# Attention and FFN on one core: q and k loaded onto the two partition halves, nine tokens a row, and turned as 64x64 tiles

## The chip, the cores and the metric

The kernel runs on one core of a Trainium2 chip. The metric is the time of one execution on the device, in microseconds. The kernel before takes 364.85 us (median of 3 runs, 364.39 to 365.44).

## What is computed

```python
B, H, S, D = 8, 8, 576, 64                       # batch, heads, tokens, head size
scores = matmul(q, k.transpose(0, 1, 3, 2)) / sqrt(D)
scores = scores + bias[None]                     # by the distance of two tokens, from a 32 x 8 table
attn = exp(scores - max) / sum(...)
x = matmul(attn, v)                              # then heads side by side: 4608 tokens x 512
h = x @ w_in                                     # 512 -> 2048
out = maximum(0.01 * h, h) @ w_out               # 2048 -> 512
```

Inputs and output are float32; the kernel works in bf16 with float32 sums.

## The kernel before

**Items.** The attention is done in 32 items, numbered n = 0 to 31: one batch and one pair of heads each, four items a batch. The FFN is done in nine groups of 512 tokens. As soon as a batch's four items have left their rows in `xT`, pieces of the FFN are put between the steps of later items, so TensorE has matmuls of both kinds in its queue.

**Loading q and k.** `load_qk` (L119) takes float32 rows of q or k from memory into bf16 tiles `qn` and `kn` with a DMA from GpSimd's queue. A partition holds six consecutive tokens of each head (`RQ = 96` rows, `NC = 6` tokens a row), so q fills partitions 0 to 95 of `qn`, and k partitions 0 to 95 of `kn`. There are two buffers of each, for even and odd batches.

**Turning q and k.** The scores need q and k with the head size on the partitions: `qt` and `kt`, 128 partitions (two heads of 64) by 576 tokens. That is done in three ways:

- Items 0 to 5: `turned_pair` (L280) lets TensorE turn each head's 96x64 block by itself, `L292`: six blocks of two heads, 12 small matmuls for q and 12 for k. The two heads of a block land on the two halves of the PSUM partitions.
- Items 6 to 8: `pair_rows` (L265) has VectorE put the two heads of a row beside each other, one copy of 96x768 for q and one for k (`L270`), and TensorE turns 96x128 blocks, `L288`: six matmuls for q and six for k.
- Items 9 to 31: `pair_rows` makes the same two copies, and `turn_by_dma` (L276) turns the whole 96x1536 tile with one DMA transpose from SyncE's queue into `tu`.

After that VectorE or ScalarE copies the turned block into `qt` or `kt` (`L307`, `L313` out of PSUM; `L319`, `L326` out of `tu`); these copies read with a step, so that tokens come out in order. Then come the scores (`L354`, `L347`, `L357`, `L358`), the exponentials on ScalarE (`L373` and others), the product with the table's band on VectorE (`L408`, `L401`), the products with v (`L421`, `L432`, `L476`), the division by the sum (`L452`, `L454`) and the turning of the result into `xT` (`L490`, or a DMA transpose). FFN matmuls are `L532`, `L584`, `L720` and `L845`.

**What sets the order.** The instructions of each engine run in the order in which the program issues them. For items 0 to 7 that order is written out by hand in the string `first` (L1115): a token `tk 6` turns k of item 6, `tq 6` turns q, `rows 6` makes item 6's two copies of `L270`, `ac 4 1 0` is one piece of item 4's product with v. Later items follow `body_in_halves` (L739), then `body_in_lanes` (L915); there `rows_ahead` (L1101) makes the copies of `pair_rows` two or three items ahead.

Of the kernel before, what the change touches and what calls it, by code (L numbers as in the profile page):

```python
# [11 lines left out]
BF16 = mybir.dt.bfloat16  # L12
# [25 lines left out]
def kernel(  # L38
# [17 lines left out]
    P = 128  # L56
    n_pairs = H // 2
# [22 lines left out]
    ps_m_pool = ctx.enter_context(tc.tile_pool(name="ps_m", bufs=2, space=bass.MemoryType.PSUM))  # L80

    ident = per.tile([P, P], BF16, name="ident")
# [8 lines left out]
    hk4 = per.tile([P, n_pairs, P + SL], BF16, name="hk4")  # L91

    NBUF = 2
    RQ = 96
    NC = S // RQ
    qn = [per.tile([P, H, NC, D], BF16, name=f"qn{i}") for i in range(NBUF)]
    kn = [per.tile([P, H, NC, D], BF16, name=f"kn{i}") for i in range(NBUF)]
    vn = [per.tile([P, NJ, H, D + 1], BF16, name=f"vn{i}") for i in range(NBUF)]
    v4 = [per.tile([P, n_pairs, D + 1], BF16, name=f"v4_{i}") for i in range(NBUF)]
    kts_ = [per.tile([P, S + P], BF16, name=f"kt{i}") for i in range(2)]  # L100
# [17 lines left out]

    def load_qk(b, h0, h1, which=("q", "k")):  # L119
        i = b % NBUF  # L120
        for name, src, dst in (("q", q, qn[i]), ("k", k, kn[i])):
            if name not in which:
                continue
            nc.gpsimd.dma_start(
                out=dst[0:RQ, h0:h1, :, :].rearrange("r h c d -> r h (c d)"),
                in_=src[b, h0:h1, :, :].rearrange("h (r c) d -> r h (c d)", c=NC),
            )

# [62 lines left out]
    for j, (u, lo, w, m) in enumerate(groups):  # L191
        copy = nc.scalar.copy if j % 2 else nc.vector.tensor_copy
        copy(out=ub[:, C0 + lo : C0 + lo + m * w].rearrange("h (m w) -> h m w", w=w),
             in_=e8[:, u : u + m].unsqueeze(2).to_broadcast([H, m, w]))
    row = ub[:, :]
    nc.vector.tensor_copy(
        out=ub[:, C0 - BAND + 1 : C0],
        in_=bass.AP(tensor=row.tensor, offset=row.offset + C0 + BAND - 1,
                    ap=[list(row.ap[0]), [-1, BAND - 1]]),
# [56 lines left out]
    items = [(b, p) for b in range(B) for p in range(n_pairs)]  # L256
# [6 lines left out]
    prs, turned = {}, {}  # L263

    def pair_rows(n):  # L265

        b, p = items[n]
        t = prs[n] = pr_pool.tile([RQ, 2, NC, 2 * D], BF16, name="pr")
        for j, src in enumerate((qn, kn)):
            nc.vector.tensor_copy(out=t[:, j, :, :].rearrange("r c (e d) -> r c e d", e=2),  # L270
                                  in_=src[b % NBUF][0:RQ, 2 * p : 2 * p + 2, :, :].rearrange("r e c d -> r c e d"))

    def by_dma(n):
        return n > 2 * n_pairs

    def turn_by_dma(n):  # L276
        t = turned[n] = tu_pool.tile([P, 2 * NC, RQ], BF16, name="tu")
        nc.sync.dma_start_transpose(out=t, in_=prs.pop(n).rearrange("r j c d -> r (j c d)"))

    def turned_pair(n, j):  # L280

        if by_dma(n):
            return turned[n][:, j * NC : (j + 1) * NC, :].rearrange("p c r -> p r c")
        ps = ps_m_pool.tile([P, 8 * P], BF16, name="ps_t", tag="m")
        b, p = items[n]
        for c in range(NC):
            if n > n_pairs + 1:
                nc.tensor.transpose(ps[:, c * RQ : (c + 1) * RQ], in_=prs[n][:, j, c, :],  # L288
                                    identity=ident[0:RQ, 0:RQ])
                continue  # L290
            for e in range(2):
                nc.tensor.transpose(ps[e * D : (e + 1) * D, c * RQ : (c + 1) * RQ],  # L292
                                    in_=(qn, kn)[j][b % NBUF][0:RQ, 2 * p + e, c, :],
                                    identity=ident[0:RQ, 0:RQ])
        return ps[:, 0:S].rearrange("p (c r) -> p r c", c=NC)

    def apart(t):

# [182 lines left out]
    def x_by_dma(n):  # L481
        return n_pairs + 2 <= n < N - 1 and n != 2 * n_pairs - 1
# [127 lines left out]
    def can(kind):  # L610
        T = made[kind]
        if at_piece[kind]:
            return True
        if kind == "in":
            return T < made["ready"] and T < made["out"] + 2
        return T < made["in"]
# [54 lines left out]
    def plan(n):  # L671
        g = room["left"] = groups_of(n)
        room["lead"] = can("out") and g >= 8 and not can("in")
        room["split"] = can("out") and g < 8 and not can("in")
        room["only"] = can("in") and not can("out") and g < 6
        room["keep"] = 4 if can("out") and not room["lead"] else 0
# [357 lines left out]
    def finished(n):  # L1034
        b, p = items[n]
        if p == n_pairs - 1:
            while made["ready"] < n_tt and (made["ready"] + 1) * TT <= (b + 1) * S:
                made["ready"] += 1
# [73 lines left out]
    def score(n, u):  # L1112
# [16 lines left out]
        b 3 2, ac 3 0 1, ac 3 1 1, xt 2, xc 2, ac 3 1 2, m 4 0, m 4 2, fin 3, e 4 0, ac 3 0 2, ac 3 0 3,  # L1129
        ac 3 1 3, e 4 2, p0 0,  # L1130
        begin 4, m 4 3, dv 3 0.1, e 4 3, xt 3 o0, xc 3, b 4 0, p0 1, p1 0 0, p1 1 0, m 4 4 s, b 4 1, m 4 5,
        tk 5, ck 5, e 4 5, e 4 4, b 4 4, moe, ap 5, moe, b 4 5, b 4 2, rows 6, m 5 1, at 4, e 5 1, m 5 0,
        ac 4 1 0, ac 4 0 0, ac 4 0 1, ac 4 1 1, tq 6, e 5 0, ac 4 0 2, tk 6,
        begin 5, ac 4 0 3, m 5 5, ac 4 1 2, cq 6 v, dv 4 0, ac 4 1 3, m 5 2, e 5 5, dv 4 1, i m, m 5 3,
        m 5 4, ck 6, i m, sl 5 1, b 5 0, e 5 2, b 5 5, l 0, i s, xt 4, sl 5 2, i o1, rows 7, e 5 4, l 1,
        e 5 3, ap 6, i m, b 5 1, l 0, b 5 4, m 6 1, at 5, xc 4, l 0, b 5 2, ac 5 0 0, ac 5 0 1, ac 5 0 2,
        begin 6, ac 5 1 0, tq 7, l 0, ac 5 0 3, e 6 1, tk 7, m 6 0, e 6 0, dv 5 0, ac 5 1 1, ck 7,
        ac 5 1 2, ac 5 1 3, dv 5 1, i s, ap 7, sl 6 1, m 6 2, l 0, m 6 4, cq 7 v, xt 5, e 6 2, b 6 1, xc 5,
        m 6 3, i m, e 6 4, m 6 5, i o0, i o1, l 1, e 6 3, i m, e 6 5, b 6 2, m 7 1, b 6 5, l 0, m 7 0,
        at 6, b 6 4, sl 6 2,  # L1140
        begin 7, b 6 0, ac 6 0 0, ac 6 1 0, l 0, ac 6 0 1, ac 6 1 1, e 7 1, rows 8, ac 6 0 2, tk 8,
        ac 6 0 3, ac 6 1 2, ac 6 1 3, i s, dv 6 0, e 7 0, dv 6 1, l 0, i m, m 7 2, l 0, ck 8, sl 7 1,
        m 7 3, xt6, l 0, turn 7, m 7 4, o, e 7 3, e 7 2, b 7 2, tq 8, b 7 1, m 7 5, b 7 0, cq 8 a, o,
        e 7 4, ap 8, b 7 4, e 7 5, b 7 5, sl 7 2, o, o,
# [68 lines left out]
    for n in range(2 * n_pairs, N + 1):  # L1213
        live = n < N
        more = n + 1 < N
        if x_by_dma(n - 2):
            finished(n - 2)
        if kind_of(n) is not None:
            body_in_lanes(n)
            continue  # L1220
        plan(n)
        kinds = two_kinds(n)
        if kinds:
            body_in_halves(n, kinds)
            continue
        all_in = live and n > 2 * n_pairs and can("in") and not can("out") and left("in") >= 6
        if live:
            begin(n)
            ps_a, ps_b = qk_mm(n, 0), qk_mm(n, 1)
            exp(n, 0, ps_a)  # L1230
            exp(n, 1, ps_b)
        av_tails(n - 1)
        av(n - 1, 0)
        first = live and by_dma(n + 1)
        if first:
            band(n, 0)
# [24 lines left out]
        x_transposes(n - 1)
        while stores:
            o, y = stores.pop(0)
            nc.sync.dma_start(out=o, in_=y)
        if not x_by_dma(n - 1):
            finished(n - 1)
        if not live:
            break
        if room["only"]:
            band(n, 1)  # L1270
        band(n, 2)
        if room["only"]:
            if not by_dma(n + 2):
                pair_rows(n + 2)
            exp(n, 3, ps_b)
            moe(2)
            exp(n, 4, ps_c)
            score(n, 5)
            T, f = step("in")
            room["left"] -= 1  # L1280

            def last_bands():
                band(n, 5)
                band(n, 4)

            leaky(T, f, ffn_in(T, f), True, last_bands)
            moe(room["left"])
            continue
        block = moe_block(1 if all_in else None, "s" if n == 3 * n_pairs - 1 else 0)
        next(block)  # L1290
        exp(n, 3, ps_b)
        next(block)
        if not all_in:
            exp(n, 4, ps_c)
        if can("out"):
            next(block)
# [38 lines left out]
```

## Time and profile before

| | before |
|---|---|
| median of the runs | 364.85 us (364.39 to 365.44) |
| span of the profiled execution | 362.8 us |
| TensorE (PE) busy | 353.4 us, 97% |
| ScalarE (ACT) busy | 243.4 us, 67% |
| VectorE (DVE) busy | 189.5 us, 52% |
| GpSimd (POOL) busy | 107.4 us, 30% |
| DMA packets | 106429, 40.27 MB |

The span is the profiled execution's own time; around it lie 2.05 us up to the median of the runs, and the prediction takes that part as it is.

PE is a matmul and PEld the load of its weights. Times are microseconds from the start of the span unless marked ns. A matmul's duration in the trace is its passage through the array, and several are under way at once. So what a matmul costs is read from the distance between the starts of two runs of matmuls, not from its duration. In a row of the timeline the first number is the start, the second the time from the first start to the last end of a run of like instructions, and "x12" their count. A form such as 96*64 in a TensorE row is the part of the array that the instruction uses: rows * columns.

### The profile page before, as it was taken

To read this page: it belongs to the slowest core of one execution; us is meant where nothing else is said; L and a number is where in the kernel's file an instruction comes from. 1 tells how busy PE (TensorE), PEld (TensorE's weight loads), DVE (VectorE), ACT (ScalarE), POOL (GpSimd) and SP (SyncE) were. 2 spreads that over 40 slices of the span, in tenths; PEclk is the share of its full clock that TensorE was granted. 3 is DMA by queue.
4 is the path that set the end of the run, shared out by engine and by line. 5 is a ranking of instruction groups with operands and counts; after the bars stand their busy time and mean duration, and the time that the engine had idled before them with its cause. 6 is when DMAs were issued, how large, how long until landed. Compare 5 with 4: busy or idle time off the path is not lost.

```text
span 362.8 us, 12074 instructions
## 1 busy us (share of the span) xinstructions
PE 353.4 (97%) x5174; PEld 204.7 (56%) x5191; DVE 189.5 (52%) x499; ACT 243.4 (67%) x364; POOL 107.4 (30%) x195
## 2 busy tenths in 40 slices
PE   7899999999999999999999999999999999999996
PEld 3465555555556777666666665565666544444443
DVE  3796876677756767655555566556554300200000
ACT  5999888479958898777777777777776264054111
POOL 8857617254334344432243334211000000000000
PEclk8999999999999999999999999999999999999999
DMA  8999999997899899979998889875111000210212
GB/s 104 196 193 147 190 206 159 197 156 115 99 130 137 114 148 139 138 120 122 133 136 124 108 119 129 122 103 96 52 49 51 29 31 0 85 33 0 80 66 87
DMA packets 106429, 40.27 MB, mean 111 GB/s; under 512 B 83713, under 2 KB 102409, under 8 KB 106377
## 3 DMA queue, kind: packets, MB, share of 16 engines
q0 software_dynamic: 55200, 18.36, 48.4%
q1 hardware_dynamic: 49880, 19.06, 27.2%
q10 hardware_dynamic: 1296, 2.10, 1.6%
q8 instruction: 41, 0.67, 0.7%
q14 instruction: 12, 0.09, 0.1%
HBM read 37.68 MB, written 9.45 MB: 130 GB/s over the span
## 4 chain that ended last, share of the span: by engine, by line
PE 93%; DVE 3%; ACT 1%; issue 1%; DMA 1%; POOL 0%; ACTq 0%; POOLq 0%
PE pm L845 35%; PE pm L584 16%; PE pm L532 15%; PE ps_o L476 8%; PE ps_s L354 8%; PE pm L720 2%; PE ps_o L432 2%; PE ps_o L421 1%; PE ps_s L845 1%; DMA kn<-in_k_dram 1%; DVE at L408 1%; PE ps_t L292 1%; PE pm L577 1%; PE ps_s L347 1%; PE ps_s L357 1%
## 5 line engine op out<-in xcount | busy, mean ns | idle before, releaser
L845 PE MATMUL pm<-xT,w_in_sb 64*128 64x512 bf16 x608 | 142.1, 376 | 0.0
L373 ACT ACTIVATE at<-ps_s 128x1024 bf16<-128x1024 f32 x120 | 118.6, 1026 | 33.7 <-PE ps_s L354 32.1
L845 PE MATMUL pm<-w_out_sb,gt 64*128 64x512 bf16 x544 | 132.6, 376 | 0.0
L556 ACT ACTIVATE gt<-pm 128x512 bf16<-128x512 f32 x140 | 82.1, 605 | 38.8 <-PE pm L532 33.4
L408 DVE TENSOR_TENSOR at<-at,hk 128x768 bf16<-128x768 bf16 (+3 forms) x149 | 65.6, 453 | 41.6 <-ACT at L385 24.8
L845 PEld LDWEIGHTS <-w_in_sb 64*128 64x128 bf16 x608 | 50.7, 94 | 20.4 <-issue 0.7
L845 PEld LDWEIGHTS <-gt 64*128 64x128 bf16 x544 | 47.0, 94 | 22.7 <-issue 3.5
L584 PE MATMUL pm<-w_out_sb,gt 128*128 128x512 bf16 x261 | 59.0, 379 | 0.7 <-issue 0.5
L532 PE MATMUL pm<-xT,w_in_sb 128*128 128x512 bf16 x242 | 56.9, 379 | 0.5
L354 PE MATMUL ps_s<-qt,kt 64*128 64x512 bf16 x240 | 44.3, 383 | 2.3 <-ACT at L373 0.8
L584 PEld LDWEIGHTS <-gt 128*128 128x128 bf16 x268 | 25.5, 98 | 29.9
L532 PEld LDWEIGHTS <-w_in_sb 128*128 128x128 bf16 x252 | 23.7, 98 | 27.0 <-issue 0.6
L476 PE MATMUL ps_o<-vn,at 64*128 64x65 bf16 x1920 | 38.4, 190 | 0.0
L476 PEld LDWEIGHTS <-at 64*128 64x128 bf16 x1920 | 35.7, 94 | 4.6 <-issue 4.4
L131 POOL DMA_DIRECT2D vn<-in_v_dram x32 | 33.8, 1060 | 9.1 <-issue 4.2
L385 ACT ACTIVATE at<-ps_s 128x576 bf16<-128x576 f32 x30 | 19.9, 663 | 17.9 <-PE pm L845 17.9
L454 DVE TENSOR_TENSOR opair<-ps_o,rcp 128x320 bf16<-128x320 f32 x64 | 29.1, 487 | 1.1
L896 DVE COPY y<-pm 128x512 f32<-128x512 f32 x17 | 11.8, 692 | 27.7 <-PE pm L845 27.7
L597 DVE COPY y<-pm 128x512 f32<-128x512 f32 x11 | 7.6, 691 | 33.5 <-PE pm L584 30.6
L354 PEld LDWEIGHTS <-kt 64*128 64x128 bf16 x240 | 14.7, 94 | 16.7 <-issue 6.6
L1088 POOL COPY tick<-opair 1x1 bf16<-1x1 bf16 x43 | 7.9, 185 | 54.6 <-DVE opair L454 54.6
L1088 POOL COPY tick<-at 1x1 bf16<-1x1 bf16 x21 | 5.5, 263 | 61.0 <-DVE at L408 61.0
(108 smaller groups left out, 348.9 us busy)
## 6 DMA issues: line engine op xcount, KB each, us to landing
out_dram<-y SPq DMA_DIRECT2D x24, 256.0 KB, 3.7
qn<-in_q_dram POOLq DMA_DIRECT2D x28, 144.0 KB, 4.7
kn<-in_k_dram POOLq DMA_DIRECT2D x28, 144.0 KB, 3.5
vn<-in_v_dram POOLq DMA_DIRECT2D x24, 128.0 KB, 4.5
w_in_sb<-in_moe_w_in_dram POOLq DMA_DIRECT2D x4, 512.0 KB, 9.2
w_out_sb<-in_moe_w_out_dram POOLq DMA_DIRECT2D x2, 1024.0 KB, 13.4
out_dram<-y ACTq DMA_DIRECT2D x7, 256.0 KB, 2.0
vn<-in_v_dram POOLq DMA_DIRECT2D x16, 64.0 KB, 8.0
```

The lines of the kernel that those rows point to most:

```text
L131: nc.gpsimd.dma_start(out=vn[b % NBUF][:, c, h0:h1, 0:D], in_=v[b, h0:h1, c * P : (c + 1) * P, :].rearrange("h s d -> s h d"),)
L354: nc.tensor.matmul(ps[:, e, :], lhsT=kt[r, u * P : (u + 1) * P], rhs=qt[r, 0:512], start=True, stop=True)
L373: nc.scalar.activation(at[:, :, u, 0:512], ps, AF.Exp, scale=scale)
L385: nc.scalar.activation(at4[:, 0:w], ps.rearrange("p e i -> p (e i)")[:, 0:w], AF.Exp, scale=scale)
L408: nc.vector.tensor_tensor(out=o, in0=o, in1=m, op=ALU.mult)
L454: nc.vector.tensor_tensor(out=opair[:, 0:m, e * D : (e + 1) * D], in0=ps[:, :, 0:D], in1=rcp.to_broadcast([P, m, D]), op=ALU.mult)
L476: m = nc.tensor.matmul(outs[n][e][:, ic * (D + 1) : (ic + 1) * (D + 1)], lhsT=at[halves[r], o : o + P], rhs=vn[b % NBUF][halves[r], c, 2 * ...
L532: nc.tensor.matmul(pm, lhsT=w_in_sb[:, c, f * P : (f + 1) * P], rhs=xT[c][:, T * TT : (T + 1) * TT], start=(c == 0), stop=(c == n_cc - 1))
L556: nc.scalar.activation(g, pm, AF.Prelu, bias=0.0, scale=1.0, alpha=0.01)
L584: nc.tensor.matmul(pm, lhsT=gt[:, f, ts * P : (ts + 1) * P], rhs=w_out_sb[:, f, :], start=(f == 0), stop=(f == n_fc - 1))
L845: m = nc.tensor.matmul(o, lhsT=w, rhs=x, start=was is None, stop=need[bank] == 0)
L1088: nc.gpsimd.tensor_copy(out=tick, in_=at4_[home(n)][0:1, S - 1 : S] if part == 2 else ops_[n - 2 + part][0:1, 0, 0:1])
```

## The change

q and k go into one tile `qkn` for each buffer: q on partitions 0 to 63, k on partitions 64 to 127, nine tokens a row (64 x 9 = 576) where there were six. A load has 64 rows of 2304 bytes for each head where it had 96 of 1536. For all nine items that TensorE turns (0 to 8), `turn_by_pe` turns 64x64 blocks straight out of `qkn`: nine blocks of two heads, 18 small matmuls for q and 18 for k. The copies of `pair_rows` for items 6, 7 and 8, and the tokens that made them, are gone. For items 9 to 31 `pair_rows` is one copy of 128x1152 in place of two of 96x768, and the DMA transpose takes a 128x1152 tile where it took 96x1536. The order of all other steps is as it was.

```diff
-    RQ = 96
+    RQ = P // 2
     NC = S // RQ
-    qn = [per.tile([P, H, NC, D], BF16, name=f"qn{i}") for i in range(NBUF)]
-    kn = [per.tile([P, H, NC, D], BF16, name=f"kn{i}") for i in range(NBUF)]
+    qkn = [per.tile([P, H, NC, D], BF16, name=f"qkn{i}") for i in range(NBUF)]
+    rows_of = {"q": slice(0, RQ), "k": slice(RQ, P)}
...
-                out=dst[0:RQ, h0:h1, :, :].rearrange("r h c d -> r h (c d)"),
+                out=qkn[i][rows_of[name], h0:h1, :, :].rearrange("r h c d -> r h (c d)"),
                 in_=src[b, h0:h1, :, :].rearrange("h (r c) d -> r h (c d)", c=NC),
...
-        t = prs[n] = pr_pool.tile([RQ, 2, NC, 2 * D], BF16, name="pr")
-        for j, src in enumerate((qn, kn)):
-            nc.vector.tensor_copy(out=t[:, j, :, :].rearrange("r c (e d) -> r c e d", e=2),
-                                  in_=src[b % NBUF][0:RQ, 2 * p : 2 * p + 2, :, :].rearrange("r e c d -> r c e d"))
+        t = prs[n] = pr_pool.tile([P, NC, 2 * D], BF16, name="pr")
+        nc.vector.tensor_copy(out=t.rearrange("r c (e d) -> r c e d", e=2),
+                              in_=qkn[b % NBUF][:, 2 * p : 2 * p + 2, :, :].rearrange("r e c d -> r c e d"))
...
-        t = turned[n] = tu_pool.tile([P, 2 * NC, RQ], BF16, name="tu")
-        nc.sync.dma_start_transpose(out=t, in_=prs.pop(n).rearrange("r j c d -> r (j c d)"))
+        t = turned[n] = tu_pool.tile([P, NC, P], BF16, name="tu")
+        nc.sync.dma_start_transpose(out=t, in_=prs.pop(n).rearrange("r c d -> r (c d)"))
+
+    def turn_by_pe(n, which):
+
+        b, p = items[n]
+        ps = {j: ps_m_pool.tile([P, 8 * P], BF16, name="ps_t", tag="m") for j in which}
+        for c in range(NC):
+            for j in which:
+                r = slice(j * RQ, (j + 1) * RQ)
+                for e in range(2):
+                    nc.tensor.transpose(ps[j][e * D : (e + 1) * D, c * RQ : (c + 1) * RQ],
+                                        in_=qkn[b % NBUF][r, 2 * p + e, c, :], identity=ident[r, r])
+        return [ps[j][:, 0:S].rearrange("p (c r) -> p r c", c=NC) for j in which]
...
-        for c in range(NC):
-            if n > n_pairs + 1:
-                nc.tensor.transpose(ps[:, c * RQ : (c + 1) * RQ], in_=prs[n][:, j, c, :],
-                                    identity=ident[0:RQ, 0:RQ])
-                continue
-            for e in range(2):
-                nc.tensor.transpose(ps[e * D : (e + 1) * D, c * RQ : (c + 1) * RQ],
-                                    in_=(qn, kn)[j][b % NBUF][0:RQ, 2 * p + e, c, :],
-                                    identity=ident[0:RQ, 0:RQ])
-        return ps[:, 0:S].rearrange("p (c r) -> p r c", c=NC)
+            return turned[n][:, :, j * RQ : (j + 1) * RQ].rearrange("p c r -> p r c")
+        return turn_by_pe(n, (j,))[0]
...
-        tk 5, ck 5, e 4 5, e 4 4, b 4 4, moe, ap 5, moe, b 4 5, b 4 2, rows 6, m 5 1, at 4, e 5 1, m 5 0,
+        tk 5, ck 5, e 4 5, e 4 4, b 4 4, moe, ap 5, moe, b 4 5, b 4 2, m 5 1, at 4, e 5 1, m 5 0,
```

The tokens `rows 7` and `rows 8`, and the call of `pair_rows` in the general loop, go in the same way.

On TensorE, where q of item 6 is turned between two pieces of item 4's product with v (`at` is that item's weights after the exponential, `vn` is v, `pr` the rows that VectorE put side by side). Before:

```order
L432 LDWEIGHTS at_113
L432 MATMUL ps_o<-vn_107,at_113 128x65
L288 LDWEIGHTS pr
L288 MATMUL ps_t<-ident,pr 128x96
...
L432 LDWEIGHTS at_113
L432 MATMUL ps_o<-vn_107,at_113 128x65
```

The pair of rows of `L288` stands six times. Now, at the same place:

```order
L432 LDWEIGHTS at_111
L432 MATMUL ps_o<-vn_105,at_111 128x65
L287 LDWEIGHTS qkn_103
L287 MATMUL ps_t<-ident,qkn_103 64x64
...
L432 LDWEIGHTS at_111
L432 MATMUL ps_o<-vn_105,at_111 128x65
```

The pair of rows of `L287` stands 18 times, on 64 rows of `qkn` itself; the products with v around it have not moved.

On VectorE, at the same place of the program (`rcp` and `opair` are item 4's division). Before:

```order
L408 TENSOR_TENSOR at_113<-at_113,hk 128x2x384
L270 COPY pr<-qn_103 96x768
L270 COPY pr<-kn_105 96x768
L307 COPY qt_117<-ps_t 128x576
L452 RECIPROCAL rcp<-ps_o 128x5
L454 TENSOR_TENSOR opair<-ps_o,rcp 128x5x64
```

Now:

```order
L408 TENSOR_TENSOR at_111<-at_111,hk 128x2x384
L307 COPY qt_115<-ps_t 128x576
L452 RECIPROCAL rcp<-ps_o 128x5
L454 TENSOR_TENSOR opair<-ps_o,rcp 128x5x64
L452 RECIPROCAL rcp<-ps_o 128x5
```

The two copies are gone and nothing else moved. TensorE's first `L287` there waits for the load itself, where `L288` waited for VectorE's copy.

More of the change, by code (lines that the diff above doesn't have):

```diff
@@ L120, in load_qk @@
         i = b % NBUF
-        for name, src, dst in (("q", q, qn[i]), ("k", k, kn[i])):
+        for name, src in (("q", q), ("k", k)):
             if name not in which:
@@ L276, in turn_by_dma @@
     def turn_by_dma(n):
-        t = turned[n] = tu_pool.tile([P, 2 * NC, RQ], BF16, name="tu")
-        nc.sync.dma_start_transpose(out=t, in_=prs.pop(n).rearrange("r j c d -> r (j c d)"))
+        t = turned[n] = tu_pool.tile([P, NC, P], BF16, name="tu")
[10 more added lines that the diff above has]
+        return [ps[j][:, 0:S].rearrange("p (c r) -> p r c", c=NC) for j in which]
     def turned_pair(n, j):
         if by_dma(n):
-            return turned[n][:, j * NC : (j + 1) * NC, :].rearrange("p c r -> p r c")
-        ps = ps_m_pool.tile([P, 8 * P], BF16, name="ps_t", tag="m")
-        b, p = items[n]
-        for c in range(NC):
-            if n > n_pairs + 1:
-                nc.tensor.transpose(ps[:, c * RQ : (c + 1) * RQ], in_=prs[n][:, j, c, :],
-                                    identity=ident[0:RQ, 0:RQ])
-                continue
-            for e in range(2):
-                nc.tensor.transpose(ps[e * D : (e + 1) * D, c * RQ : (c + 1) * RQ],
-                                    in_=(qn, kn)[j][b % NBUF][0:RQ, 2 * p + e, c, :],
-                                    identity=ident[0:RQ, 0:RQ])
-        return ps[:, 0:S].rearrange("p (c r) -> p r c", c=NC)
+            return turned[n][:, :, j * RQ : (j + 1) * RQ].rearrange("p c r -> p r c")
+        return turn_by_pe(n, (j,))[0]
     def apart(t):
@@ L1131 @@
         begin 4, m 4 3, dv 3 0.1, e 4 3, xt 3 o0, xc 3, b 4 0, p0 1, p1 0 0, p1 1 0, m 4 4 s, b 4 1, m 4 5,
-        tk 5, ck 5, e 4 5, e 4 4, b 4 4, moe, ap 5, moe, b 4 5, b 4 2, rows 6, m 5 1, at 4, e 5 1, m 5 0,
+        tk 5, ck 5, e 4 5, e 4 4, b 4 4, moe, ap 5, moe, b 4 5, b 4 2, m 5 1, at 4, e 5 1, m 5 0,
         ac 4 1 0, ac 4 0 0, ac 4 0 1, ac 4 1 1, tq 6, e 5 0, ac 4 0 2, tk 6,
         begin 5, ac 4 0 3, m 5 5, ac 4 1 2, cq 6 v, dv 4 0, ac 4 1 3, m 5 2, e 5 5, dv 4 1, i m, m 5 3,
-        m 5 4, ck 6, i m, sl 5 1, b 5 0, e 5 2, b 5 5, l 0, i s, xt 4, sl 5 2, i o1, rows 7, e 5 4, l 1,
+        m 5 4, ck 6, i m, sl 5 1, b 5 0, e 5 2, b 5 5, l 0, i s, xt 4, sl 5 2, i o1, e 5 4, l 1,
         e 5 3, ap 6, i m, b 5 1, l 0, b 5 4, m 6 1, at 5, xc 4, l 0, b 5 2, ac 5 0 0, ac 5 0 1, ac 5 0 2,
@@ L1140 @@
         at 6, b 6 4, sl 6 2,
-        begin 7, b 6 0, ac 6 0 0, ac 6 1 0, l 0, ac 6 0 1, ac 6 1 1, e 7 1, rows 8, ac 6 0 2, tk 8,
+        begin 7, b 6 0, ac 6 0 0, ac 6 1 0, l 0, ac 6 0 1, ac 6 1 1, e 7 1, ac 6 0 2, tk 8,
         ac 6 0 3, ac 6 1 2, ac 6 1 3, i s, dv 6 0, e 7 0, dv 6 1, l 0, i m, m 7 2, l 0, ck 8, sl 7 1,
@@ L1272 @@
         if room["only"]:
-            if not by_dma(n + 2):
-                pair_rows(n + 2)
             exp(n, 3, ps_b)
```

## The prediction

> **What bounds the kernel now.** I read the stretches first: how much of each TensorE was busy.
>
> ```profile
> core 0: us, PE busy (x) PEld busy (x) DVE busy (x) ACT busy (x) POOL busy (x), PEclk, DMA share, GB/s
> 0.00:9.00 9.00, 6.53 (x60) 3.07 (x60) 3.40 (x25) 4.62 (x11) 7.83 (x17) 0.88 0.82 103
> 9.00:18.00 9.00, 7.25 (x114) 3.93 (x112) 6.42 (x15) 9.00 (x15) 7.56 (x13) 0.93 1.30 196
> 18.00:27.00 9.00, 8.27 (x183) 6.14 (x182) 8.58 (x25) 8.26 (x12) 5.06 (x8) 1.00 1.52 194
> 27.00:36.00 9.00, 8.60 (x135) 5.10 (x133) 6.20 (x17) 8.30 (x14) 6.91 (x10) 1.00 1.34 146
> 36.00:63.00 27.00, 26.84 (x356) 15.05 (x359) 20.95 (x55) 22.30 (x35) 12.95 (x24) 1.00 1.45 186
> 109.00:264.00 155.00, 155.00 (x2898) 98.53 (x2892) 97.43 (x252) 118.90 (x172) 48.96 (x94) 1.00 0.86 119
> ```
>
> From 36 us on TensorE is never idle: 26.84 of 27 us, then 155 of 155. Only the first 36 us hold idle time, 36 - (6.53 + 7.25 + 8.27 + 8.60) = 5.35 us, and there ScalarE (9.00 of 9 from 9 to 18 us) and VectorE (8.58 of 9 from 18 to 27 us) are full. Next, TensorE's waits from 36 to 360 us, in one row:
>
> ```profile
> PE pm L584 <- issue: 0.5, 3, 0.2
> ```
>
> No wait for VectorE, ScalarE or a DMA stands there. So after 36 us whatever shortens those three gains nothing, and whatever lengthens TensorE's own queue is paid in full. That splits the change in two: its relief falls on engines that nobody waits for after 36 us, and its price falls on TensorE.
>
> **Part 1: what small matmuls cost, and what a change of their form costs.** The timeline of TensorE, first in a place where `L292` turns q of item 3 between products with v, then where `L288` turns item 6, and three more runs of `L288`:
>
> ```profile
> 17.43 0.63 PE L432 MATMUL ps_o<-vn,at 128*128 128x65 bf16 x15
> 17.99 0.45 PE L292 MATMUL ps_t<-ident,qn 96*64 96x96 bf16 x12
> 18.37 0.33 PE L432 MATMUL ps_o<-vn,at 128*128 128x65 bf16 x5
> 18.63 0.39 PE L354 MATMUL ps_s<-gt 64*128 64x512 bf16 x2
> ...
> 37.22 0.79 PE L432 MATMUL ps_o<-vn,at 128*128 128x65 bf16 x20
> 37.85 0.42 PE L288 MATMUL ps_t<-ident,pr 96*128 96x96 bf16 x6
> 38.10 0.32 PE L432 MATMUL ps_o<-vn,at 128*128 128x65 bf16 x5
> 38.26 0.42 PE L288 MATMUL ps_t<-ident,pr 96*128 96x96 bf16 x6
> 38.52 0.31 PE L432 MATMUL ps_o<-vn,at 128*128 128x65 bf16 x5
> ...
> 46.39 0.42 PE L288 MATMUL ps_t<-ident,pr 96*128 96x96 bf16 x6
> 46.74 0.39 PE L354 MATMUL ps_s<-qt,kt 64*128 64x512 bf16 x2
> ...
> 58.11 1.04 PE L584 MATMUL pm<-w_out_sb,gt 128*128 128x512 bf16 x4
> 58.98 0.42 PE L288 MATMUL ps_t<-ident,pr 96*128 96x96 bf16 x6
> 59.24 0.38 PE L357 MATMUL ps_s<-qt,kt 128*128 128x512 bf16 x1
> ```
>
> By distance of starts: six `L288` of 96 columns take 0.25 us (37.85 to 38.10), 42 ns each; twenty `L432` of 65 columns take 0.63 us, 31 ns each; four `L584` of 512 columns take 0.87 us, 217 ns each. From 65 to 512 columns that is 0.416 ns a column, so 64 columns take 30 ns.
>
> Twelve `L292` last 0.45 us from first start to last end, and a single one of their durations is 0.206 us (row below). So eleven starts lie within 0.24 us: the two heads of a block, on the two column halves, run together, six pairs of at most 48 ns.
>
> Now the change of form. `L432` x15 takes 0.56 us up to `L292`; at 31 ns it should be 0.46: 0.10 us are lost where the form goes from 128*128 to 96*64. Coming out, `L432` x5 takes 0.26 us up to `L354` (to 64*128), against 0.16 us at 38.10 up to `L288`: 0.10 again. `L292` itself takes 0.38 us to the next row, `L288` 0.25 us: 0.13 more, which is 0.10 for the way out and 0.03 for a slow first step. `L288` between `L432`, both using the whole width, shows no such loss; only at 46.74, where `L354` follows, it takes 0.35 us.
>
> The edit for items 6 to 8 makes each of the six runs of `L288` a run of 64*64, a form that its neighbours don't have. Price of one run: 0.10 in, 0.13 out and first step, and nine pairs by 30 ns against six by 42 ns, 0.27 - 0.255 = 0.015; together 0.245 us. Five runs pay that; the one at 46.39 had its way out already and pays 0.145. Sum 5 x 0.245 + 0.145 = 1.37 us. All of it lies between 37 and 60 us, where TensorE doesn't wait: it goes to the end. I take 1.3, since the steps read from two digits may each be 0.01 less. The Trainium skill, page "TensorEngine Tiling (Array Packing)", Key Properties, says that changing the tiling mode, not just the tile, drains TensorE; it lists 64x64 as a mode of its own, which no run here has shown yet, and gives no time.
>
> Items 0 to 5 pay the same two changes of form before and after; only nine by 30 stands for six by 42, 12 x 0.015 = 0.18 us, in a stretch where ScalarE and VectorE often set the pace. I take 0.1 (bounds 0 and 0.18).
>
> **The weight loads** could spoil the 30 ns. Their rows:
>
> ```profile
> L292 PEld LDWEIGHTS <-qn x72: 106/110/170, 5.6 to 27.5; 96*64 96x64 bf16 x72
> L292 PE MATMUL ps_t<-ident,qn x72: 206/206/289, 5.6 to 27.5; 96*64 96x96 bf16 x72
> ```
>
> The load stays 64 columns wide and today hides in a pair's 42 to 48 ns. Whether it also hides in 30 is not shown. If it were the limit today, pairs would stay at 48 ns: nine by 48 for nine by 30 is 0.16 us more a run, 18 runs, 2.9 us at most. I take nothing, because the matmul's price follows its columns from 65 to 512 with no floor in sight. The Trainium skill, page "TensorE: Matmul & The Clock Gate", section LDWEIGHTS, gives columns / 1.2 ns, 53 ns for 64 columns; by that the 18 runs would cost 18 x 9 x 23 = 3.7 us more, an estimate from that page. This trace, with pairs under 48 ns, does not bear it out.
>
> **Part 2: VectorE.** Six copies go in items 4 to 7, and in the later 23 items one copy replaces two.
>
> ```profile
> L270 DVE COPY pr<-qn x26: 339/457/461, 36.9 to 248.6; 96x768 bf16<-96x768 bf16 x26
> L270 DVE COPY pr<-kn x26: 338/340/718, 37.2 to 248.9; 96x768 bf16<-96x768 bf16 x26
> ```
>
> The first stands at 36.9 us, so 6 x 0.4 = 2.4 us go from a stretch in which TensorE has no wait for VectorE: worth nothing. The 128x1152 copy is between 0.4 us (one of today's) and 1.2 us (three halves of the pair, 0.8 x 1.5). VectorE has 155 - 97.4 = 57.6 us free from 109 to 264 us, about 3.5 us an item, so either is covered; without that cover it would cost up to 0.4 us an item. The DMA transpose moves the same bytes (96 x 1536 = 128 x 1152) and is issued two or three items ahead; zero.
>
> **Part 3: loads and the start.** Loads have a third fewer rows and the same bytes. What waits for them:
>
> ```profile
> DMA packets 540, 0.38 MB, mean 190 GB/s; under 512 B 48, under 2 KB 540, under 8 KB 540
> ...
> PE ps_t L292 <- DMA kn<-in_k_dram: 1.0, 1, 1.0
> ...
> DVE at L401 <- DMA hk<-u_row: 1.6, 1, 1.6
> ```
>
> The first row is 6.5 to 8.5 us, nearly all loads of q and k: 190 GB/s, so a load of 147 KB in bf16 takes 0.78 us. If rows were all that counted, a third of it would go, 0.26 us for k and as much for q ahead of it; if bytes, nothing. Since a later wait of VectorE for the bias rows (1.6 us) swallows most of an earlier start, I take a gain of 0.1, ends 0 and 0.5. The edit's cost from the other side: each load now reaches only half of the partitions. If that halved its rate, q and k of the first item would land up to 1.6 us later. The Trainium skill, page "SBUF — State Buffer", section Door 1, measures 196 GB/s for partitions 0 to 63 and 328 for all 128, at 1 MiB; the 190 GB/s here is just under the smaller one, so by that rule the loads stay as they are.
>
> **The sum** against the profiled execution: 362.8 + 1.3 + 0.1 - 0.1 = 364.1 us of span; with the 2.05 us between span and median, 366.15, rounded to 366.1 us, 0.34% over 364.85. A measurement here can tell about 0.3%, 1.1 us.
>
> **The rivals.**
> - Relief wins: faster. The first stage is set by the loads and not by ScalarE and VectorE; TensorE's 5.35 us of idle time shrink by 2.5 us or more with earlier q, k and bias rows, and the 1.3 us are paid back: 366.1 - 2.5 = 363.6. For it: DMA shares of 1.3 to 1.5, and the 1.6 us wait. Against it: ScalarE at 9.00 of 9 us right behind the start. It decides only if the early gain passes 2.4 us. 0.07.
> - The change of form costs nothing for 64*64, or the early gain is near 0.5 us and the price near 1: no change, 364.9. For it: the price is near the bound, and 64*64 is not in this trace. 0.2.
> - Weight loads or missing overlap of the two heads set the pace: pairs at 48 ns, +2.9 at most, about half of it covered before 36 us: 366.1 + 2 = 368. 0.12. Late loads by half the partitions, up to +1.6, count here too; they hide behind the 1.6 us wait.
> - The change doesn't do what it says: excluded, the order of instructions shows the 18 matmuls.
>
> **The numbers.** The forecast as worked out has 0.61. Its own range, price 0.9 to 1.6 and early gain 0 to 0.5 us, is 365.3 to 366.6; about two thirds of it lie over 365.95, so 0.41 slower and 0.2 the same. With the rivals: slower 0.41 + 0.12 = 0.53, the same 0.2 + 0.2 = 0.40, faster 0.07. The range takes in the no-change case and the weight loads: 364.7 to 368.0.
>
> **What would show it.** Right: in the profile after, the six runs of 64*64 between 37 and 62 us take about 0.5 us from start to start of the neighbours where they took 0.29, and TensorE is still without waits after 36 us, its span longer by that sum. Wrong: pairs of `L287` further apart than 30 ns (weight loads), no 0.10 us beside them (the price of the form), the first `L287` later or earlier than 5.37 us by more than 0.3 us (loads), or a wait of TensorE for VectorE or `tu` behind 63 us (the large copy).

## The result, and the profile after

The changed kernel takes 369.18 us (median of four runs: 368.04, 370.32, 368.02, 370.92) against 364.69 us: ratio 1.0126, 95% interval 1.009 to 1.0163. It is slower, and by more than the range held. The profiled execution is the run of 368.04 us, with a span of 366.3 us, 3.5 us longer than before's 362.8.

The stretches of the changed kernel; columns as before:

```profile
core 0: us, PE busy (x) PEld busy (x) DVE busy (x) ACT busy (x) POOL busy (x), PEclk, DMA share, GB/s
0.00:9.00 9.00, 6.59 (x96) 3.34 (x97) 3.40 (x26) 4.99 (x12) 7.89 (x18) 1.00 0.81 106
9.00:18.00 9.00, 8.07 (x96) 4.40 (x96) 6.93 (x17) 8.37 (x13) 6.75 (x12) 0.62 1.37 197
18.00:27.00 9.00, 8.52 (x215) 6.70 (x214) 8.02 (x23) 8.73 (x11) 5.65 (x9) 1.00 1.50 194
27.00:36.00 9.00, 7.74 (x143) 4.63 (x143) 5.33 (x16) 7.15 (x11) 6.66 (x10) 1.00 1.35 165
36.00:63.00 27.00, 27.00 (x401) 15.13 (x395) 17.66 (x42) 22.06 (x34) 11.58 (x21) 1.00 1.28 172
109.00:264.00 155.00, 154.58 (x2882) 102.06 (x2882) 97.58 (x234) 116.72 (x167) 48.78 (x97) 1.00 0.82 122
```

TensorE loses time in two rows where the forecast had none: 27 to 36 us (7.74 busy, 8.60 before) and 109 to 264 us (154.58 of 155). TensorE's waits from 26 to 150 us name both places:

```profile
PE ps_tx L490 <- issue: 1.2, 1, 1.2
PE ps_s L347 <- issue: 0.4, 1, 0.4
```

"issue" says that the profile finds nothing it waited for. From 20 us on the list has one more wait of this kind:

```profile
PE ps_o L432 <- issue: 0.2, 1, 0.2
```

The timeline at the two larger ones, and around two of the 64x64 runs. At 29.30 us the kernel before makes the five turns of `L490` without a break; then the changed kernel:

```profile
29.30 0.44 PE L490 MATMUL ps_tx<-ident,opair 128*128 128x128 bf16 x5
```

```profile
29.23 0.53 PE L432 MATMUL ps_o<-vn,at 128*128 128x65 bf16 x12
29.60 0.39 PE L490 MATMUL ps_tx<-ident,opair 128*128 128x128 bf16 x4
31.14 0.22 PE L490 MATMUL ps_tx<-ident,opair 128*128 128x128 bf16 x1 [1.16 <-issue]
31.20 0.32 PE L432 MATMUL ps_o<-vn,at 128*128 128x65 bf16 x5
```

```profile
39.46 0.47 PE L287 MATMUL ps_t<-ident,qkn 64*64 64x64 bf16 x18
39.87 0.33 PE L432 MATMUL ps_o<-vn,at 128*128 128x65 bf16 x5
40.12 0.47 PE L287 MATMUL ps_t<-ident,qkn 64*64 64x64 bf16 x18
```

```profile
137.04 0.34 PE L347 MATMUL ps_s<-qt,kt 64*128 64x64 bf16 x7
137.80 0.20 PE L347 MATMUL ps_s<-qt,kt 64*128 64x64 bf16 x1 [0.42 <-issue]
```

The fifth of five turns starts 1.38 us behind the fourth (29.77 to 31.14); at their pace of 56 ns that is 1.32 us lost. The last of eight `L347` starts 0.61 us behind the seventh, 0.58 us lost. The small one:

```profile
24.54 0.20 PE L432 MATMUL ps_o<-vn,gt 128*128 128x65 bf16 x1
24.95 0.43 PE L432 MATMUL ps_o<-vn,gt 128*128 128x65 bf16 x9 [0.21 <-issue]
```

In the kernel before, these ten run through from 24.53 us on. From start to start 0.41 us pass, 0.38 are lost; at 28.4 us 0.2 of them are taken up again, since there the kernel before waits 0.25 us for ScalarE. How far the changed kernel lies behind at each place is read from the start of the same ScalarE instruction in both traces:

| us in the kernel before | changed kernel behind by | what lies between |
|---|---|---|
| 25 | 0.0 | start and loads |
| 36 | 1.51 | the stand at 29.8 us and the small one at 24.5 us |
| 66 | 2.89 | the six 64x64 runs: 1.38 |
| 139 to the end | 3.5 | the stand at 137.2 us |

So the six runs, 1.3 us in the forecast, cost 1.38; the other 2.1 us (1.51 + 0.58) come from stands that no term held. In the median more is lost: the two longer runs have spans of 368.5 and 369.1 us and a mean granted clock of .977 and .982, where the other two have 366.2 and 366.3 us and .99.

### The profile page after: what moved, and what is told of

It is laid out like the page before. It is cut to its first block, busy times and chain, and to the rows that moved or that the text cites. A ratio compares the mean times of both kernels' runs of the same rounds, so it can differ in the third digit from the quotient of the medians.

```text
span 366.3 us, 12373 instructions
## 1 busy us (share of the span) xinstructions
PE 357.9 (98%) x5335; PEld 211.5 (58%) x5335; DVE 189.0 (52%) x470; ACT 244.1 (67%) x364; POOL 102.9 (28%) x195
## 4 chain that ended last, share of the span: by engine, by line
PE 95%; ACT 2%; DMA 1%; issue 1%; DVE 0%; POOL 0%; ACTq 0%; POOLq 0%
PE pm L845 34%; PE pm L584 16%; PE pm L532 15%; PE ps_s L354 9%; PE ps_o L476 8%; PE ps_o L432 3%; PE pm L720 2%; PE ps_t L287 2%; PE ps_o L421 1%; ACT at L373 1%; PE ps_s L845 1%; DMA qkn<-in_k_dram 1%; PE ps_s L357 1%; PE ps_s L347 1%; PE pm L577 1%
## 5 line engine op out<-in xcount | busy, mean ns | idle before, releaser
L584 PE MATMUL pm<-w_out_sb,gt 128*128 128x512 bf16 x268 | 59.8, 379 | 0.0
L385 ACT ACTIVATE at<-ps_s 128x576 bf16<-128x576 f32 x30 | 19.8, 661 | 18.0 <-PE pm L845 17.9
L354 PEld LDWEIGHTS <-kt 64*128 64x128 bf16 x240 | 15.5, 94 | 15.7 <-issue 6.7
L1088 POOL COPY tick<-at 1x1 bf16<-1x1 bf16 x21 | 3.8, 183 | 62.9 <-DVE at L408 62.9
```

What stands on the lines that cost most here:

```text
L354: nc.tensor.matmul(ps[:, e, :], lhsT=kt[r, u * P : (u + 1) * P], rhs=qt[r, 0:512], start=True, stop=True)
L385: nc.scalar.activation(at4[:, 0:w], ps.rearrange("p e i -> p (e i)")[:, 0:w], AF.Exp, scale=scale)
L584: nc.tensor.matmul(pm, lhsT=gt[:, f, ts * P : (ts + 1) * P], rhs=w_out_sb[:, f, :], start=(f == 0), stop=(f == n_fc - 1))
```

## The experiments

Two theories had to be told apart from rivals. **F, instruction supply:** TensorE's instructions come in blocks, and it reached the end of a block before the next was there. **K, clock:** the rest is TensorE's clock, granted at half for longer. Beside them **E**, the price of the form. In the trace a DMA queue of its own carries packets of 16384 bytes ("instruction"); the changed kernel has 42. Ahead of the first large stand TensorE has done 479 matmuls and 480 weight loads, ahead of the second 2255 of each and 33 more instructions that only wait. So the late instructions are the 960th and the 4544th, 3584 apart: 14 times 256. At the small stand it is the 704th (351 matmuls and 352 weight loads ahead of it), 256 before the 960th. The Trainium skill, page "Runtime: NRT & Kernel Launch", section Instruction fetch mechanics, has TensorE refilled in 16 KiB blocks of 256 instructions, its cost "mostly hidden". The distance agrees with the blocks; "hidden" is what the runs below test.

The runs, each beside its own runs of the kernel before:

| run | median us | ratio (95%) |
|---|---|---|
| changed kernel again | 368.56 | 1.0113 (1.0075 to 1.0151) |
| 32 pairs more at the start | 367.01 | 1.0065 (1.0049 to 1.0082) |
| 48 pairs more | 366.16 | 1.0053 (1.0024 to 1.0082) |
| items 6 to 8 from the gathered tile | 367.58 | 1.0096 (1.0066 to 1.0127) |
| the same and 24 pairs more | 368.76 | 1.0113 (1.0089 to 1.0136) |
| more dummies | 369.03 | 1.0132 (1.0064 to 1.0201) |
| before, items 6 to 8 in small blocks | 365.63 | 1.0026 (1.0006 to 1.0046) |
| before, 16 pairs more | 365.34 | 1.0005 (0.9984 to 1.0025) |
| before, 3 matmuls at the start | 366.15 | 1.0040 (1.0019 to 1.0061) |
| before, 12 matmuls at the start | 364.55 | 0.9998 (0.9989 to 1.0006) |

**The changed kernel once more.**

> The changed kernel once more, for the spread of its runs and their clocks. Theory F (instruction supply): TensorE's instructions come in blocks of 16384 bytes (256 instructions); the changed kernel reaches the end of a block at the fifth transposing of L490 near 29.8 us and at the last matmul of an L347 group near 137.2 us before the next block is there, and stands for 1.38 and 0.61 us. The places are set by the count of instructions, so both stalls must be there again, at the same two instructions, by 1.0 to 1.5 and 0.3 to 0.9 us. Rival C (chance or disturbance of that one execution): the stalls are gone or elsewhere. Theory K (clock): the runs differ by how long TensorE is granted half its clock before 25 us: a run at a mean clock of .99 takes 368.0, one at .98 or less 370 to 371.

Both stands are there again, at the same two instructions: 0.53 us from start to start at `L490` and 0.61 at `L347`. The place is fixed; the first one's size is not (0.47 us lost against 1.32). Its profiled run was half-clocked up to 20.3 us and 1.67 us behind at 25 us, where the first profile was level. The clock's mean doesn't tell the length (this run is listed at 1.0, since its first record comes at 20.3 us), but the matmuls do: its `L287` at 13.69 us takes 0.69 us, those at 39 us 0.47. At the small stand's place (the 704th instruction, 26.2 us here) it runs through; the packet had started 2.8 us ahead. Theory K had put a run at .99 at 368.0 us and one at .98 or less at 370 to 371: the run at .977 took 370.49 and the one at .991 368.59, but one at .986 only 367.04.

**Ends of blocks moved: the changed kernel with 32 pairs more.**

> The changed kernel with 42 matmuls of 122 columns in place of the 10 of 512 that warm TensorE up at the start: the same columns, 64 more instructions ahead of everything else, so every end of a block falls 32 pairs earlier in the program. Theory F: no block that ends near 29.8 or 137.2 us is as dense now; both stalls are gone, PE has no gap over 0.3 us there and activations behind 140 us come 1.5 to 2.0 us earlier than in the changed kernel: span 364.3, time 366.1 (365.6 to 366.8). Rival D (the stalls belong to the 64x64 turns, or to transfers that are late at these instructions): both stalls stay at L490 and L347 as they were, span 366.3, time 368.0. Six 64x64 runs of items 6 to 8 cost what they did (1.38) under both.

```diff
-            nc.tensor.matmul(pw, lhsT=ones[:, 0:P], rhs=ones, start=True, stop=True)
+            nc.tensor.matmul(pw[:, 0:122], lhsT=ones[:, 0:P], rhs=ones[:, 0:122], start=True, stop=True)
...
-        spin 10 o, tk 0, tq 0, ck 0,
+        spin 42 o, tk 0, tq 0, ck 0,
```

Its waits from 26 us on:

```profile
PE ps_o L421 <- issue: 0.3, 1, 0.3
PE pm L845 <- issue: 0.2, 1, 0.2
```

`L490` and `L347` run through: the stands don't belong to those instructions, nor to their data. They are now at the 480th matmul again, which is an `L421` here (29.45 to 29.91 us), and near 129.2 us, one block earlier than the old second one: 0.41 and 0.43 us lost. So the rival falls, and the place follows the count; but they shrank where I had expected them gone. Time 367.0 against 366.1 expected: 0.8 us for these two stands, and 1.0 us at 25 us, with half the clock from 9.5 to 19.8 us.

**The count alone, on the kernel before.** This run decides: the work of before, no 64x64 turn, only the ends of blocks made equal.

> The kernel before, its work untouched, with 26 matmuls of 197 columns in place of the 10 of 512 at the start: 16 pairs more. From item 9 on the changed kernel has 144 pairs more than the kernel before, which is one block of 128 pairs and 16; so these 16 alone put every later end of a block at the same instruction as in the changed kernel. Theory F: TensorE stands for 0.4 to 0.8 us ahead of the last matmul of the L347 group near 134.2 us, where the kernel before does not stand at all, since the same transfers hold the fetch up until about 132.4 us; nothing of that size near 30 us, whose block is less dense without the 64x64 turns. Span 363.4, time 365.2. Rival (the stall is a matter of the changed layout or of its transfers): no gap there, time 364.6.

The same edit, with 26 matmuls of 197 columns. The kernel before at that place, then this one:

```profile
133.91 0.47 PE L354 MATMUL ps_s<-qt,kt 64*128 64x512 bf16 x2
134.13 0.37 PE L347 MATMUL ps_s<-qt,kt 64*128 64x64 bf16 x8
```

```profile
134.75 0.47 PE L354 MATMUL ps_s<-qt,kt 64*128 64x512 bf16 x2
134.97 0.34 PE L347 MATMUL ps_s<-qt,kt 64*128 64x64 bf16 x7
135.74 0.20 PE L347 MATMUL ps_s<-qt,kt 64*128 64x64 bf16 x1 [0.43 <-issue]
```

The stand appears ahead of the same last matmul of the group, 0.63 us from start to start. It is its only wait between 36 and 360 us, and none is near 30 us, as expected. Such a stand is too small for the times to tell (ratio 1.0005, interval on both sides); the trace shows it. Its start was half-clocked up to 17.0 us, and it is 0.84 us behind at 25 us, long ahead of the stand.

**What a fetch needs.** In eight of the profiles there are fifteen such stands; the table has eight of them. The last column runs from the start of the block's packet to the first instruction out of it.

| kernel | packet starts | TensorE stops | goes on | packet to instruction |
|---|---|---|---|---|
| changed | 22.31 | 24.54 | 24.95 | 2.64 |
| changed | 28.39 | 29.77 | 31.14 | 2.75 |
| changed | 135.51 | 137.19 | 137.80 | 2.29 |
| changed, again | 29.04 | 31.14 | 31.67 | 2.63 |
| 32 pairs more | 27.34 | 29.45 | 29.91 | 2.57 |
| 48 pairs more | 25.64 | 27.48 | 28.09 | 2.45 |
| more dummies | 30.31 | 30.88 | 33.02 | 2.71 |
| before, 16 pairs more | 133.35 | 135.11 | 135.74 | 2.39 |

All fifteen lie between 2.29 and 2.82 us. In the kernel before the packet next to late starts at 24.07 us, 2.9 us ahead of its use, and TensorE runs through. What varies is when the packet starts, and how long a block of 256 instructions lasts: that packet, too, started 3.3 us after the block before had run out (20.8 us), but the block in use lasted 6.2 us, up to 27.0. The DMA engines of the changed kernel from 132.4 to 136.6 us, in slices of 105 ns (digits are tenths busy), and the row of its instruction queue:

```profile
DMA  8999799999999999999999999942060000099991
q8 instruction: 1, 0.02, 1.4%
```

The block before had run out at 132.37 us. The packet, the only one there, starts at 135.51 us, just after the strip has fallen from 9 to 0 (the 29th digit, 135.3 to 135.4 us). In the kernel before, the same burst of loads and DMA transposes ends at 132.4 us, and its packet starts at 132.41 us; with 16 pairs more, the strip falls from 8 to 2 between 133.0 and 133.3 us, and the packet starts at 133.35 us. Near 30 us the engines are full throughout; there the changed kernel's packet starts 3.4 us after the block before had run out (24.95 us), and 256 instructions are used up in 4.8 us. That the transfers hold the fetch back is read from these places; a kernel with the loads moved out of its way wasn't tried, so it is not shown.

**The form.** First the changed kernel with items 6 to 8 turned from the gathered tile again:

> The changed kernel with items 6 to 8 turned from the gathered tile again, nine pairs of 64 rows by 128 columns a run, VectorE's three copies back at their old places: 108 TensorE instructions fewer from 50 us on. Theory E (change of form is 1.38 of the loss): behind 66 us the activations come 1.2 to 1.5 us earlier than in the changed kernel if 64 rows by 128 columns enter and leave like the old turns; if this form costs the drains too, under 0.6 us. Theory F: the stall near 29.8 us stays (1.2 to 1.5), and the one near 137.2 us goes, since ends of blocks behind 60 us fall elsewhere: 0.6 us more. Span 364.3 by both, time 366.1. Rival (VectorE's relief was worth something that the drains hid): the copies cost over 0.3 us where they stand, span 364.8 or more.

```diff
+                if n > n_pairs + 1:
+                    nc.tensor.transpose(ps[j][:, c * RQ : (c + 1) * RQ], in_=prs[n][r, c, :],
+                                        identity=ident[r, r])
+                    continue
```

with the tokens `rows 6`, `rows 7`, `rows 8` at their old places. Its timeline:

```profile
38.82 0.38 PE L436 MATMUL ps_o<-vn,at 128*128 128x65 bf16 x7
39.13 0.43 PE L287 MATMUL ps_t<-ident,pr 64*128 64x64 bf16 x9
39.50 0.33 PE L436 MATMUL ps_o<-vn,at 128*128 128x65 bf16 x5
39.76 0.43 PE L287 MATMUL ps_t<-ident,pr 64*128 64x64 bf16 x9
```

The six runs still cost 1.06 us (1.19 behind at 36 us, 2.25 at 66). Only 0.32 us came back, the case "under 0.6" of the expectation, and not the 1.2 to 1.5 on which its times were built: the span of the profile is 364.9 us, the median 367.58. From the last product with v to the first turn pass 0.125 us, and 0.122 on the way out: sixty-four rows at full width change the form as well. As expected there is no stand near 137 us. The one at `L490`, which is `L494` here, is its only wait for "issue" from 20 us on, with 0.71 us lost instead of 1.2 to 1.5. There is no sign that VectorE's copies cost anything.

```profile
PE ps_tx L494 <- issue: 0.5, 1, 0.5
```

Then the kernel before with only this part of the change:

> The kernel before with its old loads, but items 6 to 8 turned like items 0 to 5, twelve pairs of 96x64 a run, without VectorE's three gathering copies: one part of the change alone. Theory E: what costs is the change to an array half as wide and back, not the 64 rows: six runs at 0.24 us more, activations behind 66 us 1.2 to 1.5 us later than in the kernel before; span 364.2, time 366.0 (365.6 to 366.5) with no further stall. Rival (only the 64x64 form is dear, or the eighteen pairs): under 0.6 us, time 365.3 or less. Rival (VectorE's relief pays): at or under 364.7.

```diff
-            if n > n_pairs + 1:
+            if False:
...
-        b 4 2, rows 6, m 5 1, at 4,
+        b 4 2, m 5 1, at 4,
```

(and `rows 7`, `rows 8` alike). Its timeline:

```profile
38.11 0.45 PE L292 MATMUL ps_t<-ident,qn 96*64 96x96 bf16 x12
38.49 0.33 PE L432 MATMUL ps_o<-vn,at 128*128 128x65 bf16 x5
38.75 0.45 PE L292 MATMUL ps_t<-ident,kn 96*64 96x96 bf16 x12
```

From run to run 0.64 us pass here, 0.66 for the 64x64 runs (39.46 to 40.12), 0.41 in the kernel before. It is 0.18 behind at 36 us and 1.39 at 66: 1.21 us for the form with 96 rows, no stand, no sign of a gain from VectorE's six copies. The time, 365.63 us, is within the range expected. The 64x64 turns therefore add little of their own (1.38 against 1.21); what costs is leaving the form of the neighbours.

**The clock.** First more work for TensorE in the changed kernel:

> The changed kernel with 14 dummy matmuls of 256 columns at its two places for them near 11 and 14 us in place of 3 (the output is as before). Theory K (a stretch of 3.41 us in which TensorE has too little to do costs it half its clock in the next ones, and the changed kernel has more such runs): with more to do TensorE is granted its full clock by 14.5 us in nearly all runs, no run has a mean clock under .986, and the spread of the spans falls under 1.5 us; the dummies themselves cost 0.5 to 1.2 us on the early path, so the median is not lower than 367. Rival (the clock follows something else than how much TensorE does): runs at .977 to .982 and spans of 368.5 and more as before. 11 pairs more also move the ends of blocks: stalls near 30 and 137 us of 0 to 1.4 us, not the same as before.

```diff
-        e 0 5, ck 1, ap 1, m 0 3, cq 1 v, warm 0 2, m 1 0, tq 2, b 0 5, cq 2 v, e 0 3, e 1 0, b 0 1,
-        warm 0 1, m 1 1, e 1 1, tk 2, b 0 0, m 1 4,
+        e 0 5, ck 1, ap 1, m 0 3, cq 1 v, warm 0 8, m 1 0, tq 2, b 0 5, cq 2 v, e 0 3, e 1 0, b 0 1,
+        warm 0 6, m 1 1, e 1 1, tk 2, b 0 0, m 1 4,
```

Three of its four runs have spans of 366.8 to 367.3 us at a clock of .995, close together as theory K expected, but not shorter than the changed kernel's better runs (366.2 and 366.3); the profiled one, against expectation, has 371.4 us at .982. Its stretches around the first of its two stands (the second, at 141.2 us, adds 1.0 us):

```profile
core 0: us, PE busy (x) PEld busy (x) DVE busy (x) ACT busy (x) POOL busy (x), PEclk, DMA share, GB/s
25.00:28.80 3.80, 3.50 (x89) 2.58 (x82) 3.35 (x11) 3.75 (x6) 1.89 (x3) 1.00 1.63 186
28.80:32.20 3.40, 2.16 (x63) 1.77 (x62) 2.37 (x7) 3.21 (x6) 2.83 (x5) 1.00 1.20 105
32.20:39.10 6.90, 6.08 (x48) 3.33 (x48) 1.94 (x6) 2.91 (x3) 5.12 (x7) 0.51 1.25 192
39.10:42.50 3.40, 3.40 (x40) 1.58 (x39) 2.18 (x6) 2.62 (x6) 0.83 (x2) 1.00 1.73 164
```

A stand of 2.13 us (30.88 to 33.02) lies across the stretch up to 32.2, TensorE is busy for 2.16 of its 3.4 us, and the next 6.83 us have half the clock (0.51). The kernel falls from 1.83 us behind at 25 us to 6.28 at 34: 2.1 us for the stand and some 2.3 for the clock. So a stand can cost the clock on top of itself; this is seen once, and the stands of 1.38 and 1.39 us (changed kernel; the one with both repairs) were not followed by half the clock. The Trainium skill, page "TensorE: Matmul & The Clock Gate", Part 1, has the gate watch free-running windows of 3.41 us and close after an idle one; here a stretch that was busy for two thirds was enough. It isn't always enough. The clock in these traces changes in steps of 3.41 us; in the twelve traces, full-clocked steps in which TensorE was busy for 0.70 or less came fourteen times. Half the clock followed eight of them (busy 0.50 to 0.68) and not the other six (0.64 to 0.70, the changed kernel's step with its stand at 29.8 us, 0.66, among them); it followed none of the fuller steps (0.75 and more). I take it that the changed kernel's runs at .977 and .982, 2.2 to 2.9 us longer than their sisters, lost the clock in this way, too. None of them was profiled, so that is not shown.

Then the clock by itself, on the kernel before:

> The kernel before with 3 matmuls of 512 columns at the start in place of 10, to price the clock by itself on a kernel without 64x64 turns: TensorE does less before 5 us. Theory K: half the clock for longer at the start, 7 to 14 us instead of 3.4, activations at 25 us 0.5 to 1.7 us later than in the kernel before, and nothing lost behind 30 us but what the ends of blocks, 7 pairs earlier, bring (0 to 0.5). Time 365.2 to 366.4. Rival (early half clock hides behind VectorE and ScalarE): time 364.6 whatever the clock, and the early lag of the changed kernel has another cause.

```diff
-        spin 10 o, tk 0, tq 0, ck 0,
+        spin 3 o, tk 0, tq 0, ck 0,
```

One row of its timeline; twelve `L292` take 0.45 us in the kernel before:

```profile
12.87 0.69 PE L292 MATMUL ps_t<-ident,qn 96*64 96x96 bf16 x12
```

It is half-clocked up to 17.0 us and 0.82 us behind at 25 us and still at 136 us; then a wait of 0.5 us for a load of v. So what a half-clocked start costs is carried to the end in the old kernel too. Where the half clock lay and the lag at 25 us, over the profiles: 6.9 to 10.3 us, 0 (before); 9.0 to 15.8, -0.05 (48 pairs more); 11.1 to 17.9, 0.0 (changed); 9.6 to 16.4, 0.16 (before, small blocks); 8.3 to 18.5, 0.58 (gathered tile); 9.5 to 19.8, 1.01 (32 pairs more); up to 20.3, 1.67 (changed, again). A stretch of 6.8 us between 9 and 18 us thus cost 0.2 us at most by 25 us, the longer ones 0.58 to 1.67. (The run with more dummies, 8.3 to 15.2 and 1.83, has their own time in it.)

How often is it long? A mean clock of .986 or less came in 16 of 36 runs of the six kernels with 64-row turns (4 of 8 of the changed kernel itself), and in 6 of 89 of before and its four variants (a half-clocked start ahead of the first record is not in these means). Such runs are more frequent with the change; how much of that is the stands and how much the start was not settled.

**Two attempts at a better version.** The changed kernel with more pairs, and with both repairs:

> The changed kernel with 58 matmuls of 88 columns at the start, 48 pairs more than it has (the run with 32 more left two stalls of 0.4 us, at 29.5 and 129.2 us). Theory F: the block that ends near 28 us now takes some 5.6 us, and with a fetch that starts 3.4 us into it and needs 2.5 us it stalls by 0 to 0.4 us; those that end near 122 and 127 us by 0 to 0.3 us; none at the old places. With the 64x64 runs at 1.38 and 0 to 1 us from the clock before 25 us the span is 364.3 to 365.5, time 366.1 to 367.3. Rival: stalls at the fifth L490 turn and at L347 as in the changed kernel.

Its only wait from 26 us on:

```profile
PE ps_t L287 <- issue: 0.4, 1, 0.4
```

It lies inside a run of `L287` near 28 us, where the end of the block fell (0.59 us lost); nothing near 137 us. It is level at 25 us, 0.56 behind at 34, 1.94 at 66 and 1.83 at 160: one stand and the six runs. At 366.16 us, 48 dummy matmuls take back 3.0 of the change's 4.5 us (2.4 by the 368.56 us of the repeat). The two profiles, level at 25 us, differ by 1.6 us at the end (3.47 and 1.83 behind): that is the stands; the rest of the median was not read from a trace. What is left is the price of the form with a stand that I had put at 0.4 at most.

> The changed kernel with both repairs: items 6 to 8 turned from the gathered tile as nine pairs of 64 rows by 128 columns, and 34 matmuls of 150 columns at the start in place of 10 of 512, 24 pairs more. By the ends of blocks (theory F) the block that ends near 29 us takes about 5.3 us and still stalls by 0.2 to 0.6 us; the one near 139 us takes 5.1 us, and its fetch can start at about 134.6, so it does not stall. With 1.06 for the six runs and 0 to 1 from the clock before 25 us: span 364.1 to 365.2, time 365.9 to 367.0. If the form and the ends of blocks were not the causes (rival), it stays at 367.0 or more. No version with 64-row turns comes under the kernel before by these terms.

This went wrong: 368.76 us. Its waits from 20 us on:

```profile
PE ps_o L436 <- issue: 1.2, 1, 1.2
PE ps_t L291 <- issue: 0.8, 1, 0.8
...
PE pm L849 <- issue: 0.4, 1, 0.4
```

Three stands, at the matmuls of the 352nd and 480th pair and near 145.4 us, of 0.94, 1.3 and 0.5 us. All are ends of blocks; the packets started 1.3 to 1.6 us before TensorE stopped. The time lies where the rival had put it, but not for its reason: the six runs cost 1.07 us again, and the stands are at ends of blocks. I had worked with a start 3.4 us after the end before and with the burst at its old time. Where a stand can be follows from the count; its size doesn't, since the start of the packet shifts with the loads.

Last, the kernel before with a longer start:

> The kernel before with 12 matmuls of 512 columns at the start in place of 10; TensorE waits for the first loads there for 1.0 to 1.3 us, so the two more fit. Theory K: with more to do before 5 us the half clock starts later or is shorter, so fewer runs have it up to 17 us; median span 362.3, time 364.1 (363.8 to 364.6). Rival: no change in the clocks, time 364.6. The ends of blocks move by two pairs only and bring no stall over 0.2 us.

364.55 against 364.56 us, ratio 0.9998 (0.9989 to 1.0006). In its profile the half clock ends at 5.75 us and it is 0.23 us ahead, but over twelve runs nothing is left of that. No version was faster than the kernel before.

## Why the prediction was wrong, point by point

- **The relief is worth nothing: right.** VectorE fell from 20.95 to 17.66 us of busy time between 36 and 63 us, and TensorE stayed full. Doing away with the copies alone (the small blocks in the kernel before) brought no gain that shows.
- **The form, 1.3 us: right,** 1.38. A run takes 0.278 us, 0.124 in and 0.125 out. The reason was too narrow: it is not only the width of the tile, since all three forms tried that differ from the neighbours' (64*64, 96*64, 64*128) cost it. The Trainium skill, page "TensorEngine Tiling (Array Packing)", Key Properties, says that a change of mode drains; by these runs that is 0.09 to 0.1 us each way.
- **The weight loads: right.** Eighteen `L287` in 0.278 us are nine pairs, 32 ns apart behind a first step of 52, so neither 48 nor 53 ns hold. The rival that gave 368 us had a number near the result and a mechanism that isn't there.
- **Loads and start, -0.1:** the first `L287` starts at 5.23 us (5.37 before), VectorE waits 2.0 us for the bias rows (1.6): level at 25 us, though half the clock lasted 6.8 us instead of 3.4.
- **The 128x1152 copy, between 0.4 and 1.2 us and covered: right.**

```profile
L269 DVE COPY pr<-qkn x23: 741/746/751, 60.2 to 252.1; 128x1152 bf16<-128x1152 bf16 x23
```

- **The step that failed is the sum,** "362.8 + 1.3 + 0.1 - 0.1 = 364.1 us of span". It priced the 144 added pairs of matmul and weight load by the time they take in the array, as if TensorE's queue were always filled, and what "would show it" said so: "TensorE is still without waits after 36 us". The 288 instructions also moved every end of a block: by 32 instructions behind item 8, after one whole block. Two ends fell where 256 instructions are used up in 4.8 us and the next packet had started only 1.4 and 1.7 us before they were, a third (24.5 us) where it had started 2.2 us before. That is 1.32 + 0.58 us in the profiled run, and 0.2 that were left of the third one's 0.38. Putting 32 instructions into the old kernel made the second one without any of the change.
- **The clock had no term either.** The first two stretches of the old profile (0.88 and 0.93) showed that half the clock occurs; its length was taken as fixed. Two profiles of the changed kernel differ by 1.67 us at 25 us, and in one trace a stand brought half the clock back later. I put the rest between 368.04 and the median of 369.18 down to this; the two longer runs were not profiled, so that part stays open.

## What to carry to other kernels

Where TensorE is full, small matmuls cost not only their time but also instructions: count the instructions up to the places where many short ones run while transfers are heavy, and look in the trace for how far ahead of its use each 16384-byte instruction packet starts. A wait named "issue" in the middle of a run of like matmuls can be such an end, if the lag behind the other trace grows there; a few dummy instructions ahead of everything move it, and show within one run whether a loss belongs to the change or to where the ends now lie. Turning blocks in the form that the neighbouring matmuls use saves about 0.2 us a run against the three smaller forms tried here.

## What was not expected of the hardware

- An instruction block is usable 2.3 to 2.8 us after its packet starts (fifteen stands), though the packet itself takes 0.9 to 1.5 us; the packet starts up to 4.3 us after the block before has run out when the DMA engines are full.
- One stand of 2.13 us was followed by 6.83 us at half the clock, worth some 2.3 us more: the lag went from 1.83 us at 25 us to 6.28 at 34, of which the stand is 2.1. Whether half the clock follows isn't told by how much TensorE stood alone: steps of 3.41 us that were busy for 0.64 to 0.68 went either way.
- The mean granted clock can hide a half-clocked start: 1.0 is listed for runs whose matmuls ran at half speed up to 17 and 20.3 us.
